# Attention over two K/V caches: the second cache's output weights in 128 partitions by heads, two more K tiles in halves, and the end of the last V reordered

## The chip, the cores and the metric

One core of one Trainium2 chip. The time is device microseconds (us) of a run. The kernel before takes 2613.69 us (median of 4 runs, 2612.04 to 2615.51). Each run lists its granted clock, and all profiles used here were taken in the fast state. In the profile, PE is the matmul engine, PEld its weight loads, DVE is VectorE, ACT is ScalarE, and SPq is the queue from which all large transfers are issued.

## The reference, cut to what matters

Two independent decode steps, A and B, with one query token and caches of their own. Each does:

```python
B, Sq, D = 8, 1, 1024;  H, Sk, Dh = 32, 4096, 128
q = (x @ wq).reshape(B, Sq, H, Dh).transpose(0, 2, 1, 3)
scores = einsum("bhqd,bhkd->bhqk", q, k_cache) * Dh ** -0.5
p = softmax(scores)
o = einsum("bhqk,bhkd->bhqd", p, v_cache)
out = o.transpose(0, 2, 1, 3).reshape(B, Sq, H * Dh) @ wo      # wo: 4096 x 1024
# result: concatenate([A's out, B's out], axis=-1)
```

Every byte of K and V is read once: 1074 MB, plus 34 MB of weights. All inputs are bfloat16.

Of the kernel before, what the change touches and what calls it, by code (L numbers as in the profile page):

```python
# [5 lines left out]
ALU = mybir.AluOpType  # L6
AX = mybir.AxisListType
BF16 = mybir.dt.bfloat16
FP32 = mybir.dt.float32
# [80 lines left out]
def _build_kernel(nc, caches, out):  # L90
# [6 lines left out]
    HQ = 8  # L97
# [16 lines left out]
    with es:  # L114
# [19 lines left out]
        pe = sb("pe", [128, T], BF16)  # L134
        PM = sb("PM", [128, T, HQ], BF16)
        accS = sb("accS", [128, 512], BF16)
        rl = sb("rl", [128, B], FP32)
        rl8 = sb("rl8", [128, B * HQ], FP32)
        on_sb = sb("on_sb", [128, H, B], BF16)
        on8 = sb("on8", [128, HQ, B], BF16)  # L140
        orow = sb("orow", [128, DT], BF16)

        red_ps = [ps(f"red{i}") for i in range(4)]
# [41 lines left out]

        opT, opMul, opEacc, opRed, opRmax, opNgm, opExp = {}, {}, {}, {}, {}, {}, {}
        opPV, opAcc, opExt, opQb, opQbc, opQ, opQs, opLsum = {}, {}, {}, {}, {}, {}, {}, {}
        opNorm, opProj, opUse, opPM = {}, {}, {}, {}
        last = {"misc": None, "norm": None}
        outs = []  # L190

# [14 lines left out]
        put("k", 0)  # L206
        put("wq", 1, 2)
        for n in range(NQ - 1):
            if n + 2 < NQ:
                put("k", n + 1)  # L210
            else:
                put("k", n + 1, cuts=((0, NR // 2), (NR // 2, NR)))
            put("v", n, 2)

            for c in range(NC):
                if n == done_at(c, NC, HB, B) + 1:
                    put("wo", c)
                    late[n + 2] = c
        put("v", NQ - 1, cuts=((0, NR // 2),))
        put("wo8", 0, 2)  # L220
        plan.append(("v", NQ - 1, ((NR // 2, 3 * NR // 4), (3 * NR // 4, 7 * NR // 8), (7 * NR // 8, NR))))
        tenant = [None, None, ("x", 0)]
        before = []
        for kind, n, cuts in plan:
# [4 lines left out]

        def tile_of(kind, n):  # L230
            return ring[:, slot[(kind, n)], :]

        def wo_rows(c):
            return MB * (HB if c < NC - 1 else HB - 1)

        def load_tiles():
            while issued[0] < len(plan):
                kind, n, cuts = plan[issued[0]]
                prev = before[issued[0]]
                dep = None  # L240
                if prev not in (None, (kind, n)):
                    dep = opUse.get(prev)
                    if dep is None:
                        return
                to = tile_of(kind, n)
                key = ("t", slot[(kind, n)])
                if kind in ("k", "v"):
                    blk, b = divmod(n, B)
                    c, hb = divmod(blk, HB)
                    from_ = caches[c][1 if kind == "k" else 2][b, hb * HQ:(hb + 1) * HQ].rearrange("u (m t) d -> (u m) (t d)", m=MP)  # L250
                    for r0, r1 in cuts or ((0, NR),):
                        cols = slice(r0 * CT * Dh, r1 * CT * Dh)
                        op = dma(to[:, cols], from_[:, cols], (kind + "l", r0) if cuts else key, [dep])
                        for r in range(H):
                            opT[(kind, n, r)] = op
                elif kind == "wq":
                    opT[(kind, n)] = dma(to[:, 0:DC * H * Dh], caches[n][3].rearrange("(p k) n -> p (k n)", k=DC), key, [dep])
                elif kind == "wo":
                    rows = wo_rows(n)
                    opT[(kind, n)] = dma(to[0:rows, 0:H * D], caches[n][4][0:rows * H, :].rearrange("(p r) n -> p (r n)", r=H),  # L260
                                         key, [dep])
                else:
                    opT[(kind, n)] = dma(to[:, 0:HQ * D].rearrange("p (j n) -> p j n", j=HQ),
                                         caches[-1][4][(H - HQ) * Dh:, :].rearrange("(j p) n -> p j n", p=128), key, [dep])
                issued[0] += 1


# [104 lines left out]
        def make_acc(n):  # L372
            opAcc[n] = add("act", lambda e: e.activation(accS[:], pv_ps[:], ACTF.Copy), [opPV[n], _at(opExt, n - 1)])  # L373

        def last_block(n):
            return n // B == NB - 1

        def make_ext(n):
            blk, b = divmod(n, B)
            hb = blk % HB  # L380
# [9 lines left out]

            def emit_last(e):
                for i in range(4):
                    x = e.matmul(o_ps[:, HQ * b:HQ * (b + 1)], accS[:, i * 128:(i + 1) * 128],  # L393
                                 E[:, i, PH - 1:].rearrange("p (j u) -> p j u", u=PH)[:, :, 0], start=(i == 0), stop=(i == 3))
                return x
            opExt[n] = add("pe", emit_last if last_block(n) else emit,
                           [opAcc[n], c_E, opLsum.get("rl"), last["norm"]] + (list(opQs.values()) if n == 0 else []))

        def make_lsum(blk):
            hb = blk % HB  # L400

            def emit(e):
                return e.matmul(o_ps[MB * hb:MB * (hb + 1), H * B:H * B + B], own_m[:].rearrange("p j u -> p (j u)"),
                                rsum[:, blk % 2, :], start=True, stop=True, tile_position=(0, MB * hb))

            def emit_last(e):
                for j in range(HQ):
                    x = e.matmul(o_ps[:, 64 + B * j:64 + B * (j + 1)], own_m[:, j, 0:1].to_broadcast([128, 128]),
                                 rsum[:, blk % 2, :], start=True, stop=True)
                return x  # L410
            n = blk * B + B - 1
            opLsum[blk] = add("pe", emit_last if blk == NB - 1 else emit, [opExp[n], c_own, last["norm"]])
            if blk == NB - 1:
                opLsum["rl"] = add("dve", lambda e: e.reciprocal(rl8[:], o_ps[:, 64:64 + B * HQ]), [opLsum[blk]])

        def make_norm(c):
            rows = slice(0, wo_rows(c))
            rec = add("dve", lambda e: e.reciprocal(rl[rows, :], o_ps[rows, H * B:H * B + B]),
                      [opExt[done_at(c, NC, HB, B)]] + [opLsum[blk] for blk in range(c * HB, c * HB + wo_rows(c) // MB)])
            opNorm[c] = last["norm"] = add("dve", lambda e: e.tensor_tensor(  # L420
                on_sb[rows, :, :].rearrange("p r b -> p b r"), o_ps[rows, 0:H * B].rearrange("p (b r) -> p b r", b=B),
                rl[rows, :].unsqueeze(2).to_broadcast([rows.stop, B, H]), ALU.mult), [rec, opProj.get(c - 1)])

        def make_proj(c):
            w = tile_of("wo", c)
            rows = slice(0, wo_rows(c))

            def emit(e):
                for r in range(H):
                    for q in range(NT):  # L430
                        x = e.matmul(proj[32 * q:32 * q + B, 0:DT], on_sb[rows, r, :], w[rows, r * D + q * DT:r * D + (q + 1) * DT],  # L431
                                     start=(r == 0), stop=(c < NC - 1 and r == H - 1), tile_position=(0, 32 * q))
                return x
            opProj[c] = opUse[("wo", c)] = add("pe", emit, [opNorm[c], opT[("wo", c)], c_proj] + outs)
            if c < NC - 1:
                make_out(c, opProj[c])

        def make_proj_last(norm):
            w = tile_of("wo8", 0)
            alone = ("wo", NC - 1) not in slot  # L440

            def emit(e):
                for j in range(HQ):
                    for q in range(NT):
                        x = e.matmul(proj[32 * q:32 * q + B, 0:DT], on8[:, j, :], w[:, j * D + q * DT:j * D + (q + 1) * DT],
                                     start=(alone and j == 0), stop=(j == HQ - 1), tile_position=(0, 32 * q))
                return x
            make_out(NC - 1, add("pe", emit, [norm, opT[("wo8", 0)], c_proj] + outs))

        def make_out(c, dep):  # L450
            ev = add("dve", lambda e: e.tensor_copy(orow[0:96 + B, :], proj[0:96 + B, 0:DT]), [dep] + outs[1:])
# [27 lines left out]
        for s in range(NS + LAG):  # L479
# [10 lines left out]
            if r == LAG - 1 and n >= 1:  # L490
                make_pm(n - 1)
            if r == 0 and n in late:
                make_proj(late[n])
            for k in range(4):
                v = pv_at.get(divmod(s - k, NR))
                if v is None:
# [5 lines left out]
                if k == 2:  # L502
                    make_ext(v)
                if k == 3:
                    for c in range(NC):
                        if v == done_at(c, NC, HB, B):
                            make_norm(c)
            if r == 2 and n % B == 0 and n >= 1:
                make_lsum(n // B - 1)

# [12 lines left out]
        make_pm(n)  # L523
        make_lsum(NB - 1)
        for g0, g1 in ((0, 8), (8, 12), (12, 14), (14, 16)):
            make_pv(n, g0 * RG // 16, g1 * RG // 16)
        make_acc(n)
        make_ext(n)
        norm = add("dve", lambda e: e.tensor_tensor(  # L529
            on8[:].rearrange("p j b -> p b j"), o_ps[:, 0:64].rearrange("p (b j) -> p b j", b=B),  # L530
            rl8[:].rearrange("p (j b) -> p b j", b=B), ALU.mult), [opLsum["rl"], opExt[n]])
        make_proj_last(norm)
        assert issued[0] == len(plan)

        counts = P.tokens()
# [58 lines left out]
```

## The kernel before: what the change and the argument touch

The caches are cut into 64 tiles of 8 MB (n = 0 to 63; 32 for A, 32 for B): one batch and 8 heads, in 128 partitions of 64 KB each. VectorE multiplies K tile n with the query and folds it in 8 chunks; PE sums further. The softmax of tile n and PV, the product of the probabilities with V tile n, are done while tile n + 1 is worked on. There are three slots of 64 KB per partition: two for K, in turn, and one for V. A load is issued only when the slot's last tenant is used up. The plan says in what order:

```python
        for n in range(NQ - 1):                      # NQ = 64, NR = 8 chunks
            if n + 2 < NQ:
                put("k", n + 1)
            else:
                put("k", n + 1, cuts=((0, NR // 2), (NR // 2, NR)))
            put("v", n, 2)
            for c in range(NC):
                if n == done_at(c, NC, HB, B) + 1:   # n = 32 for A, 56 for B
                    put("wo", c)                     # takes a K slot
                    late[n + 2] = c
        put("v", NQ - 1, cuts=((0, NR // 2),))
        put("wo8", 0, 2)                             # takes the V slot
        plan.append(("v", NQ - 1, ((NR // 2, 3 * NR // 4), (3 * NR // 4, 7 * NR // 8), (7 * NR // 8, NR))))
```

The weights wo of B are loaded in two parts, because its last 8 heads are finished only at the very end. The first part holds 24 heads in only 96 partitions of 64 KB; A's wo holds 32 heads in 128. In `load_tiles`:

```python
                if kind in ("k", "v"):
                    # ... (from_ is the tile in HBM)
                    for r0, r1 in cuts or ((0, NR),):
                        cols = slice(r0 * CT * Dh, r1 * CT * Dh)
                        op = dma(to[:, cols], from_[:, cols], (kind + "l", r0) if cuts else key, [dep])
                        for r in range(H):                     # every chunk, whatever the piece
                            opT[(kind, n, r)] = op
                # ... (wq)
                elif kind == "wo":
                    rows = wo_rows(n)                          # 128 for A, 96 for B
                    opT[(kind, n)] = dma(to[0:rows, 0:H * D],
                        caches[n][4][0:rows * H, :].rearrange("(p r) n -> p (r n)", r=H), key, [dep])
                else:                                          # wo8: the last 8 heads, rows of 2 KB
                    opT[(kind, n)] = dma(to[:, 0:HQ * D].rearrange("p (j n) -> p j n", j=HQ),
                        caches[-1][4][(H - HQ) * Dh:, :].rearrange("(j p) n -> p j n", p=128), key, [dep])
```

The main loop puts PV of tile n beside chunk 5 of K tile n + 1 (`pv_at = {(n + 1, 5): n ...}`). The end:

```python
        n = NQ - 1
        make_pm(n)
        make_lsum(NB - 1)
        for g0, g1 in ((0, 8), (8, 12), (12, 14), (14, 16)):
            make_pv(n, g0 * RG // 16, g1 * RG // 16)   # RG = 16; waits for opT of its last chunk
        make_acc(n)
        make_ext(n)
        # ... norm, product with wo8, output
```

## Time and profile before

| what | before |
|---|---|
| median time | 2613.69 us |
| span of the profiled execution | 2611.2 us |
| read from HBM | 1107.33 MB |
| VectorE busy | 85% |
| PE busy | 47% |

First, two lines of the page of the kernel before: what the transfers moved in 40 equal slices of 65 us, and the chain of waits that ended last, by engine.

```profile
GB/s 418 434 434 434 433 433 433 432 432 433 433 432 431 433 432 433 429 428 433 432 403 435 434 434 435 431 432 432 432 433 433 432 432 432 432 304 432 426 430 292
...
DMA 52%; DVE 44%; PE 2%; issue 1%; another core or an unknown queue 0%; SPq 0%; ACT 0%; DVEq 0%
```

Nearly every slice moves about 433 GB/s. Four stand out: the first, slice 20 (403; slices are counted from 0), slice 35 (304) and the last. The table of windows of the kernel before looks into the last three. Its columns are the stretch, its length, the busy time of each engine (PE, PEld, DVE, ACT and POOL, each with its count of instructions), the granted PE clock, the busy share of the DMA engines, and GB/s. It counts a descriptor where it starts, so a short stretch can show a little more or less than was moved in it.

```profile
1360.00:1368.00 8.00, 4.11 (x65) 2.13 (x66) 3.32 (x3) 0.00 (x0) 0.00 (x0) 0.80 0.57 213
2294.00:2336.00 42.00, 14.95 (x100) 4.59 (x100) 23.61 (x19) 0.88 (x2) 0.00 (x0) 0.58 1.00 225
2370.00:2490.00 120.00, 57.77 (x336) 16.66 (x336) 107.05 (x87) 4.61 (x13) 0.00 (x0) 0.59 1.00 431
2574.00:2584.00 10.00, 7.53 (x79) 2.58 (x77) 10.00 (x9) 0.60 (x1) 0.00 (x0) 0.84 0.40 126
2584.00:2590.00 6.00, 2.75 (x8) 1.30 (x9) 3.85 (x7) 0.60 (x2) 0.00 (x0) 0.50 1.04 390
```

The second line is wo of B: the DMA engines are fully busy (1.00) and yet move 225 GB/s, half of what the third line shows for ordinary tiles. The first and fourth lines are different in kind: there the engines are idle about half of the time (0.57 and 0.40), so the queue has run dry. The last line is mostly the 2 MB part of wo in rows of 2 KB, at 390 GB/s.

The timeline of the kernel before shows who waits. Columns: start, duration, engine, line, operation, out<-in, how many; in brackets the idle time ahead of it and what ended that.

```profile
1364.45 0.33 SPq L160 DMA_DIRECT2D ring<-in_B_k_cache_dram  x1
...
2278.68 0.33 SPq L160 DMA_DIRECT2D ring<-in_B_wo_dram  x1
2281.54 2.29 DVE L311 TENSOR_TENSOR ring<-ring,qbc 128x4096 bf16<-128x4096 bf16 x1 [3.99 <-DMA ring<-in_B_k_cache_dram]
...
2319.59 0.33 SPq L160 DMA_DIRECT2D ring<-in_B_k_cache_dram  x1
...
2355.63 2.29 DVE L311 TENSOR_TENSOR ring<-ring,qbc 128x4096 bf16<-128x4096 bf16 x1 [38.02 <-DMA ring<-in_B_k_cache_dram]
...
2580.45 0.38 SPq L160 DMA_DIRECT2D ring<-in_B_wo_dram  x1
...
2600.73 5.17 PE L365 MATMUL pv<-ring,PM 128*32 128x512 bf16 x64 [8.01 <-DMA ring<-in_B_v_cache_dram]
2605.94 0.60 ACT L373 ACTIVATE accS<-pv 128x512 bf16<-128x512 f32 x1 [16.86 <-PE pv L365]
...
2607.46 1.05 PE L445 MATMUL proj<-ring,on 128*8 128x256 bf16 x32 [0.60 <-DVE on L529]
```

VectorE waits about 4 us for each K tile (here K57, at 2281.54), and 38.02 us for K58, which was queued behind wo. At the end, all 64 matmuls of PV of the last V run after its last piece has landed.

### The profile page before, as it was taken

Reading aid. Unit: us, or ns where it says so; the run is one execution under the profiler, and the core shown is the slowest. Engines: PE = TensorE matmul, PEld = TensorE weight load, DVE = VectorE, ACT = ScalarE, POOL = GpSimd, SP = SyncE. Lnnn points to the kernel's source line nnn. Section 1 sums busy time; section 2 is a strip of 40 time slices with the busy share of each in tenths; the row PEclk is TensorE's granted clock in tenths of the full one; section 3 lists DMA queues with packets and bytes.
Section 4 is the critical chain, followed back from the end, with each engine's and each line's share of the span. In section 5 each row is a group of like instructions: output and inputs, shape, how many; then the busy total and the mean of one; then the engine's idle time right before and its main releaser. Section 6 shows DMA issues by size and latency. Waiting matters only on the chain.

```text
span 2611.2 us, 18455 instructions
## 1 busy us (share of the span) xinstructions
PE 1221.1 (47%) x8046; PEld 371.0 (14%) x8046; DVE 2221.5 (85%) x1805; ACT 105.2 (4%) x273; POOL 5.7 (0%) x23
## 2 busy tenths in 40 slices
PE   2454554454454444455453544544544544533454
PEld 0111111111111111111111111111111111111111
DVE  3898889889889889889886998898898898848896
ACT  1100000000000000000000000000000000000000
POOL 0000000000000000000000000000000000000000
PEclk7665665665665665665565656656656656655666
DMA  9999999999999999999999999999999999999997
GB/s 418 434 434 434 433 433 433 432 432 433 433 432 431 433 432 433 429 428 433 432 403 435 434 434 435 431 432 432 432 433 433 432 432 432 432 304 432 426 430 292
DMA packets 20833, 1108.55 MB, mean 425 GB/s; under 512 B 2272, under 2 KB 2336, under 8 KB 3376
## 3 DMA queue, kind: packets, MB, share of 16 engines
q1 hardware_dynamic: 20656, 1107.32, 99.1%
q8 instruction: 63, 1.03, 0.2%
q14 instruction: 18, 0.15, 0.0%
q10 hardware_dynamic: 96, 0.05, 0.0%
HBM read 1107.33 MB, written 0.03 MB: 424 GB/s over the span
## 4 chain that ended last, share of the span: by engine, by line
DMA 52%; DVE 44%; PE 2%; issue 1%; another core or an unknown queue 0%; SPq 0%; ACT 0%; DVEq 0%
DMA ring<-in_B_k_cache_dram 26%; DMA ring<-in_A_k_cache_dram 25%; DVE ring L311 23%; DVE ring L316 12%; DVE s_sb L333 6%; DVE PM L353 3%; PE red L325 2%; DMA ring<-in_B_v_cache_dram 1%; DVE rmax L339 1%; PE pv L365 0%; DVE rtmp L341 0%; DVE ngm L344 0%; SPq L160 0%; DVE on_sb L420 0%
## 5 line engine op out<-in xcount | busy, mean ns | idle before, releaser
L311 DVE TENSOR_TENSOR ring<-ring,qbc 128x4096 bf16<-128x4096 bf16 x512 | 1169.3, 2284 | 351.8 <-DMA ring<-in_B_k_cache_dram 187.2
L325 PE MATMUL red<-ring,ident 128*128 128x512 bf16 x2048 | 834.4, 553 | 1334.7 <-DVE ring L316 1334.0
L316 DVE TENSOR_TENSOR ring<-ring 128x2048 bf16<-128x2048 bf16 x512 | 618.4, 1208 | 0.1
L325 PEld LDWEIGHTS red<-ring,ident 128*128 128x128 bf16 x2048 | 202.5, 120 | 1871.0 <-DVE ring L316 1606.0
L333 DVE TENSOR_REDUCE s_sb<-red 128x32 f32<-128x512 f32 x512 | 348.6, 681 | 1.4 <-PE red L325 1.4
L365 PE MATMUL pv<-ring,PM 128*32 128x512 bf16 x4096 | 320.7, 469 | 8.0 <-DMA ring<-in_B_v_cache_dram 8.0
L353 DVE TENSOR_TENSOR PM<-pe,own_h 128x2048 bf16<-128x2048 bf16 x64 | 146.2, 2284 | 0.7 <-ACT pe L347 0.7
L365 PEld LDWEIGHTS pv<-ring,PM 128*32 128x32 bf16 x4096 | 113.5, 114 | 223.2 <-issue 174.4
L347 ACT ACTIVATE pe<-s_sb,ngm 128x256 bf16<-128x256 f32 x64 | 32.5, 509 | 1032.7 <-DVE ngm L344 1032.7
L373 ACT ACTIVATE accS<-pv 128x512 bf16<-128x512 f32 x64 | 38.2, 597 | 851.5 <-PE pv L365 851.5
L301 ACT ACTIVATE qbc<-misc 128x128 bf16<-128x128 f32 x64 | 17.8, 278 | 580.5 <-PE misc L296 580.5
L386 PE MATMUL o<-accS,E 128*32 128x32 bf16 x896 | 31.7, 177 | 0.0
L386 PEld LDWEIGHTS o<-accS,E 128*32 128x32 bf16 x896 | 25.9, 94 | 23.7 <-ACT accS L373 13.1
L339 DVE TENSOR_REDUCE rmax<-s_sb 128x1 f32<-128x256 f32 x64 | 26.9, 420 | 2.2
L296 PE MATMUL misc<-q_sb,selb 8*32 8x128 bf16 x512 | 26.1, 294 | 1.2 <-ACT q_sb L284 1.2
L431 PE MATMUL proj<-ring,on_sb 128*8 128x256 bf16 (+1 forms) x256 | 12.5, 384 | 18.1 <-DMA ring<-in_B_wo_dram 16.7
L341 DVE TENSOR_SCALAR rtmp<-half,rmax 128x32 f32<-128x32 f32 x64 | 15.4, 241 | 2.3
L296 PEld LDWEIGHTS misc<-q_sb,selb 8*32 8x32 bf16 x512 | 9.3, 103 | 54.4 <-issue 54.4
L344 DVE TRANSPOSE_TENSOR_REDUCE ngm<-rtmp 128x1 f32<-128x32 f32 x64 | 13.5, 211 | 2.2
L275 PE MATMUL o<-ring,xT 128*8 128x512 bf16 x64 | 7.2, 627 | 11.0 <-DMA ring<-in_A_wq_dram 11.0
L529 DVE TENSOR_TENSOR on<-o,rl 128x64 bf16<-128x64 f32 x1 | 0.4, 436 | 13.7 <-PE o L393 13.7
L347 ACT ACTIVATION_READ_ACCUMULATOR pe<-s_sb,ngm 128x1 f32 x64 | 11.9, 187 | 0.0
(38 smaller groups left out, 56.5 us busy)
## 6 DMA issues: line engine op xcount, KB each, us to landing
ring<-in_B_k_cache_dram SPq DMA_DIRECT2D x2, 4096.0 KB, 36.7
ring<-in_B_v_cache_dram SPq DMA_DIRECT2D x1, 4096.0 KB, 32.1
ring<-in_B_wo_dram SPq DMA_DIRECT2D x1, 2048.0 KB, 10.4
ring<-in_B_v_cache_dram SPq DMA_DIRECT2D x1, 2048.0 KB, 14.8
ring<-in_B_v_cache_dram SPq DMA_DIRECT2D x2, 1024.0 KB, 17.6
ring<-in_A_k_cache_dram SPq DMA_DIRECT2D x32, 41.6
ring<-in_A_v_cache_dram SPq DMA_DIRECT2D x32, 27.4
ring<-in_B_k_cache_dram SPq DMA_DIRECT2D x31, 41.3
```

What stands on the lines that cost most here:

```text
L296: x = e.matmul(misc[32 * g:32 * (g + 1), 0:Dh], selb[rows, b, i, :], q_sb[rows, c, j * Dh:(j + 1) * Dh], start=(i == 0), stop=(i == 1), ti ...
L301: "act", lambda e: e.activation(qbc[:, n % 2, :], misc[:, 0:Dh], ACTF.Copy),
L311: opMul[s] = add("dve", lambda e: e.tensor_tensor(v, v, qbc[:, n % 2, :].unsqueeze(1).to_broadcast([128, CT, Dh]), ALU.mult), [opT[("k", n ...
L316: return add("dve", lambda e: e.tensor_tensor(v[:, :, 0:64], v[:, :, 0:64], v[:, :, 64:128], ALU.add), [opMul[s]])
L325: i = e.matmul(dst, ident[:], v[:, :, j, :], start=(j == 0), stop=(j == 3))
L333: opRed[s] = add("dve", lambda e: e.tensor_reduce(s_sb[:, n % 2, r * CT:(r + 1) * CT], red_ps[s % 4][:, :].rearrange("p (t w) -> p t w", w ...
L339: opRmax[n] = add("dve", lambda e: e.tensor_reduce(rmax[:], s_sb[:, n % 2, :], AX.X, ALU.max), [opRed[NR * n + NR - 1]])
L347: opExp[n] = add("act", lambda e: e.activation(pe[:], s_sb[:, n % 2, :], ACTF.Exp, bias=ngm[:, n % 2:n % 2 + 1], scale=scale, accum_out=rs ...
L353: opPM[n] = add("dve", lambda e: e.tensor_tensor(PM[:], pe[:].unsqueeze(2).to_broadcast([128, T, HQ]), own_h[:].unsqueeze(1).to_broadcast( ...
L365: i = e.matmul(pv_ps[32 * q:32 * (q + 1), :], PM[:, t:t + 4, :].rearrange("p t j -> p (t j)"), v[:, t * Dh:(t + 4) * Dh], start=(g == 0), ...
L373: opAcc[n] = add("act", lambda e: e.activation(accS[:], pv_ps[:], ACTF.Copy), [opPV[n], _at(opExt, n - 1)])
L386: x = e.matmul(o_ps[MB * hb:MB * (hb + 1), H * b:H * (b + 1)], E[:, i, PH - 1 - u:PH - 1 - u + MB], accS[:, i * 128 + H * u:i * 128 + H * ...
```

## The change

The intent: let B's first 24 heads of wo reach all 128 partitions (one row of 2 KB per head and partition); have the K tile beside each wo (K33, K57) begun on its first half, so that its slot is free sooner; put three quarters of the last V, not half, ahead of the last wo; and really wait for pieces singly. The core of the diff, with cuts:

```diff
-            if n + 2 < NQ:
-                put("k", n + 1)
-            else:
-                put("k", n + 1, cuts=((0, NR // 2), (NR // 2, NR)))
+            early = n == NQ - 2 or n + 1 in [done_at(c, NC, HB, B) + 2 for c in range(NC)]
+            put("k", n + 1, cuts=((0, NR // 2), (NR // 2, NR)) if early else None)
...
-        put("v", NQ - 1, cuts=((0, NR // 2),))
-        put("wo8", 0, 2)
-        plan.append(("v", NQ - 1, ((NR // 2, 3 * NR // 4), (3 * NR // 4, 7 * NR // 8), (7 * NR // 8, NR))))
+        put("v", NQ - 1, cuts=((0, NR // 2), (NR // 2, 3 * NR // 4)))
+        put("wo_last", 0, 2)
+        plan.append(("v", NQ - 1, ((3 * NR // 4, 7 * NR // 8), (7 * NR // 8, NR))))
...
-                        for r in range(H):
+                        for r in range(r0, r1):
                             opT[(kind, n, r)] = op
...
+                    heads = slice(0, H - HQ) if kind == "wo" else slice(H - HQ, H)
+                    cols = (heads.stop - heads.start) * D
+                    opT[(kind, n)] = dma(to[:, 0:cols].rearrange("p (h n) -> p h n", n=D),
+                                         caches[-1][4][heads.start * Dh:heads.stop * Dh, :].rearrange("(h p) n -> p h n", p=128), key, [dep])
...
-            make_pv(n, g0 * RG // 16, g1 * RG // 16)
+            make_pv(n, g0, g1)
```

RG is 16, so the last pair of lines changes nothing: PV was cut in the same four pieces before. What makes them wait singly is `range(r0, r1)`; before, each later piece overwrote the landing of all chunks. The rest of the diff follows from the new layout: all four head blocks of B now use the form of unpacking, sum and normalization that only the last block had.

More of the change, by code (lines that the diff above doesn't have):

```diff
@@ L136, in _build_kernel @@
         accS = sb("accS", [128, 512], BF16)
-        rl = sb("rl", [128, B], FP32)
-        rl8 = sb("rl8", [128, B * HQ], FP32)
+        rl = sb("rl", [128, B * HQ], FP32)
         on_sb = sb("on_sb", [128, H, B], BF16)
-        on8 = sb("on8", [128, HQ, B], BF16)
         orow = sb("orow", [128, DT], BF16)
@@ L187, in _build_kernel @@
         opPV, opAcc, opExt, opQb, opQbc, opQ, opQs, opLsum = {}, {}, {}, {}, {}, {}, {}, {}
-        opNorm, opProj, opUse, opPM = {}, {}, {}, {}
+        opNorm, opProj, opUse, opPM, opRl = {}, {}, {}, {}, {}
         last = {"misc": None, "norm": None}
@@ L231, in tile_of @@
             return ring[:, slot[(kind, n)], :]
-        def wo_rows(c):
-            return MB * (HB if c < NC - 1 else HB - 1)
         def load_tiles():
@@ L257, in load_tiles @@
                     opT[(kind, n)] = dma(to[:, 0:DC * H * Dh], caches[n][3].rearrange("(p k) n -> p (k n)", k=DC), key, [dep])
-                elif kind == "wo":
-                    rows = wo_rows(n)
-                    opT[(kind, n)] = dma(to[0:rows, 0:H * D], caches[n][4][0:rows * H, :].rearrange("(p r) n -> p (r n)", r=H),
-                                         key, [dep])
-                else:
-                    opT[(kind, n)] = dma(to[:, 0:HQ * D].rearrange("p (j n) -> p j n", j=HQ),
-                                         caches[-1][4][(H - HQ) * Dh:, :].rearrange("(j p) n -> p j n", p=128), key, [dep])
+                elif kind == "wo" and n < NC - 1:
+                    opT[(kind, n)] = dma(to[:, 0:H * D], caches[n][4].rearrange("(p r) n -> p (r n)", r=H), key, [dep])
+                else:
+                    heads = slice(0, H - HQ) if kind == "wo" else slice(H - HQ, H)
+                    cols = (heads.stop - heads.start) * D
+                    opT[(kind, n)] = dma(to[:, 0:cols].rearrange("p (h n) -> p h n", n=D),
+                                         caches[-1][4][heads.start * Dh:heads.stop * Dh, :].rearrange("(h p) n -> p h n", p=128), key, [dep])
                 issued[0] += 1
@@ L373, in make_acc @@
             opAcc[n] = add("act", lambda e: e.activation(accS[:], pv_ps[:], ACTF.Copy), [opPV[n], _at(opExt, n - 1)])
-        def last_block(n):
-            return n // B == NB - 1
         def make_ext(n):
@@ L392, in emit_last @@
                 for i in range(4):
-                    x = e.matmul(o_ps[:, HQ * b:HQ * (b + 1)], accS[:, i * 128:(i + 1) * 128],
+                    x = e.matmul(o_ps[:, HQ * (hb * B + b):HQ * (hb * B + b + 1)], accS[:, i * 128:(i + 1) * 128],
                                  E[:, i, PH - 1:].rearrange("p (j u) -> p j u", u=PH)[:, :, 0], start=(i == 0), stop=(i == 3))
                 return x
-            opExt[n] = add("pe", emit_last if last_block(n) else emit,
-                           [opAcc[n], c_E, opLsum.get("rl"), last["norm"]] + (list(opQs.values()) if n == 0 else []))
+            opExt[n] = add("pe", emit_last if blk // HB == NC - 1 else emit,
+                           [opAcc[n], c_E, opRl.get(blk), last["norm"]] + (list(opQs.values()) if n == 0 else []))
         def make_lsum(blk):
@@ L407, in emit_last @@
                 for j in range(HQ):
-                    x = e.matmul(o_ps[:, 64 + B * j:64 + B * (j + 1)], own_m[:, j, 0:1].to_broadcast([128, 128]),
+                    x = e.matmul(o_ps[:, HQ * B * HB + B * (HQ * hb + j):HQ * B * HB + B * (HQ * hb + j + 1)], own_m[:, j, 0:1].to_broadcast([128, 128]),
                                  rsum[:, blk % 2, :], start=True, stop=True)
@@ L411, in make_lsum @@
             n = blk * B + B - 1
-            opLsum[blk] = add("pe", emit_last if blk == NB - 1 else emit, [opExp[n], c_own, last["norm"]])
-            if blk == NB - 1:
-                opLsum["rl"] = add("dve", lambda e: e.reciprocal(rl8[:], o_ps[:, 64:64 + B * HQ]), [opLsum[blk]])
-        def make_norm(c):
-            rows = slice(0, wo_rows(c))
-            rec = add("dve", lambda e: e.reciprocal(rl[rows, :], o_ps[rows, H * B:H * B + B]),
-                      [opExt[done_at(c, NC, HB, B)]] + [opLsum[blk] for blk in range(c * HB, c * HB + wo_rows(c) // MB)])
-            opNorm[c] = last["norm"] = add("dve", lambda e: e.tensor_tensor(
-                on_sb[rows, :, :].rearrange("p r b -> p b r"), o_ps[rows, 0:H * B].rearrange("p (b r) -> p b r", b=B),
-                rl[rows, :].unsqueeze(2).to_broadcast([rows.stop, B, H]), ALU.mult), [rec, opProj.get(c - 1)])
@@ L424, in make_proj, with make_norm @@
-        def make_proj(c):
-            w = tile_of("wo", c)
-            rows = slice(0, wo_rows(c))
+            c = blk // HB
+            opLsum[blk] = add("pe", emit_last if c == NC - 1 else emit, [opExp[n], c_own, last["norm"]])
+            if c == NC - 1:
+                k = HQ * B
+                opRl[blk] = add("dve", lambda e: e.reciprocal(rl[:], o_ps[:, (HB + hb) * k:(HB + hb + 1) * k]), [opLsum[blk]])
+        def make_norm(c, n):
+            if c < NC - 1:
+                rec = add("dve", lambda e: e.reciprocal(rl[:, 0:B], o_ps[:, H * B:H * B + B]),
+                          [opExt[n]] + [opLsum[blk] for blk in range(c * HB, (c + 1) * HB)])
+                opNorm[c] = last["norm"] = add("dve", lambda e: e.tensor_tensor(
+                    on_sb[:].rearrange("p r b -> p b r"), o_ps[:, 0:H * B].rearrange("p (b r) -> p b r", b=B),
+                    rl[:, 0:B].unsqueeze(2).to_broadcast([128, B, H]), ALU.mult), [rec, opProj.get(c - 1)])
+                return
+            hb = n // B % HB
+            k = HQ * B
+            opNorm[(c, hb)] = last["norm"] = add("dve", lambda e: e.tensor_tensor(
+                on_sb[:, HQ * hb:HQ * (hb + 1), :].rearrange("p j b -> p b j"),
+                o_ps[:, hb * k:(hb + 1) * k].rearrange("p (b j) -> p b j", b=B),
+                rl[:].rearrange("p (j b) -> p b j", b=B), ALU.mult), [opRl[n // B], opExt[n], opProj.get(c - 1)])
@@ new lines, in make_proj @@
+        def make_proj(c, heads=None):
+            if c < NC - 1:
+                w, key, norm, steps, end, first = tile_of("wo", c), ("wo", c), opNorm[c], range(H), True, True
+            else:
+                kind = "wo" if heads.start == 0 else "wo_last"
+                norm = opNorm[(c, heads.stop // HQ - 1)]
+                key = (kind, c if kind == "wo" else 0)
+                w, steps, end = tile_of(*key), heads, heads.stop == H
+                first = heads.start == 0 or HB == 1
@@ L428, in emit @@
             def emit(e):
-                for r in range(H):
+                for r in steps:
                     for q in range(NT):
-                        x = e.matmul(proj[32 * q:32 * q + B, 0:DT], on_sb[rows, r, :], w[rows, r * D + q * DT:r * D + (q + 1) * DT],
-                                     start=(r == 0), stop=(c < NC - 1 and r == H - 1), tile_position=(0, 32 * q))
-                return x
-            opProj[c] = opUse[("wo", c)] = add("pe", emit, [opNorm[c], opT[("wo", c)], c_proj] + outs)
@@ L435, in make_proj @@
-            if c < NC - 1:
+                        col = (r - steps.start) * D + q * DT
+                        x = e.matmul(proj[32 * q:32 * q + B, 0:DT], on_sb[:, r, :], w[:, col:col + DT],
+                                     start=(first and r == steps.start), stop=(end and r == H - 1), tile_position=(0, 32 * q))
+                return x
+            opProj[c] = opUse[key] = add("pe", emit, [norm, opT[key], c_proj] + outs)
+            if end:
                 make_out(c, opProj[c])
-        def make_proj_last(norm):
-            w = tile_of("wo8", 0)
-            alone = ("wo", NC - 1) not in slot
-            def emit(e):
-                for j in range(HQ):
-                    for q in range(NT):
-                        x = e.matmul(proj[32 * q:32 * q + B, 0:DT], on8[:, j, :], w[:, j * D + q * DT:j * D + (q + 1) * DT],
-                                     start=(alone and j == 0), stop=(j == HQ - 1), tile_position=(0, 32 * q))
-                return x
-            make_out(NC - 1, add("pe", emit, [norm, opT[("wo8", 0)], c_proj] + outs))
@@ L492, in _build_kernel @@
             if r == 0 and n in late:
-                make_proj(late[n])
+                make_proj(late[n], range(0, H - HQ))
             for k in range(4):
@@ L504, in _build_kernel @@
                 if k == 3:
-                    for c in range(NC):
-                        if v == done_at(c, NC, HB, B):
-                            make_norm(c)
+                    c = v // B // HB
+                    if v == done_at(c, NC, HB, B) or (c == NC - 1 and v % B == B - 1):
+                        make_norm(c, v)
             if r == 2 and n % B == 0 and n >= 1:
@@ L525, in _build_kernel @@
         for g0, g1 in ((0, 8), (8, 12), (12, 14), (14, 16)):
-            make_pv(n, g0 * RG // 16, g1 * RG // 16)
+            make_pv(n, g0, g1)
         make_acc(n)
         make_ext(n)
-        norm = add("dve", lambda e: e.tensor_tensor(
-            on8[:].rearrange("p j b -> p b j"), o_ps[:, 0:64].rearrange("p (b j) -> p b j", b=B),
-            rl8[:].rearrange("p (j b) -> p b j", b=B), ALU.mult), [opLsum["rl"], opExt[n]])
-        make_proj_last(norm)
+        make_norm(NC - 1, n)
+        make_proj(NC - 1, range(H - HQ, H))
         assert issued[0] == len(plan)
```

## The prediction

> **What bounds the kernel now.** Transfers. The page's slices show about 433 GB/s almost everywhere; VectorE idles about 4 us per K tile (4.0 us before the tile that lands at 2281.5, released by its DMA). Time is saved only where transfers run below 433 GB/s. The table of windows shows three such places besides the start:
>
> 1. 2294–2336 us: 225 GB/s. This is wo of the second cache, 96 partitions of 64 KB: (433-225)x42/433 = 20 us lost. VectorE idles from 2317.6 to 2355.6, until the next K tile lands. The Trainium skill ("SBUF — State Buffer", "Door 1: The DMA port swizzle") says that DMA bandwidth depends on how many of 16 ports the partitions reach, and that 0..63 reach only the 8 even ones. The trace agrees in kind: half rate here, full rate for the first cache's wo in 128 partitions.
> 2. 1360–1368 us: 213 GB/s, 4 us lost. The first cache's wo takes a K slot and the next K is issued late (1364.45): the queue has run dry.
> 3. 2574–2584 us: 126 GB/s, 7 us lost. The last 2 MB of wo wait for the slot of the next to last V, free at 2580.45, while the queue holds only half of the last V before it.
>
> After the last V piece lands (2600.6) comes a bare tail of 10.5 us, of which PV of the whole last V is 5.2: each piece's landing overwrites that of all chunks, so K halves and V pieces aren't waited for singly.
>
> **What the change does.**
> - wo of 24 heads goes into 128 partitions, in rows of 2 KB. The old 2 MB block has such rows already: 390 GB/s in 2584–2590. I estimate 6.3 MB in 15.5–16.5 us in place of about 35. K58's issue then waits for K57's use; with K57 in halves VectorE starts it 4 us sooner and frees it at about 2315, as wo ends. Gain 18.5 us.
> - K33 in halves: VectorE starts up to 5 us sooner, the next K is issued at about 1360. Gain 3 us.
> - K63 in halves, three quarters of the last V before the last wo: the slot is free at 2576, the queue holds work until 2584, the hole vanishes. Gain 6.5 us.
> - PV by pieces: after the last piece 8 of 64 matmuls are left, 0.7 of 5.2 us. Gain 4.5 us.
> - Added: per block 16 small sum matmuls (3.6 us of PE), a reciprocal (0.56) and a multiply (0.44), three times more; hidden in the slack.
>
> Sum 32.5 us, all on the critical path: what follows each place is bound by transfers and only shifts.
>
> **Predicted: 2581 us**, 8 in 10 between 2575 and 2589. Faster by over 2%: 0.02; within 2%: 0.97; slower: 0.01.
>
> **What would show it.** Windows: wo of the second cache at about 400 GB/s and 16 us long; VectorE's wait for the next K about 20 us in place of 38; Timeline at the end: the wo piece issued about 26 us after the last K lands, no hole in the transfers, PV of the last V in four stretches, last landing to end about 6 us.
>
> **What would make it wrong.** 2 KB rows slower over 3072 descriptors than over 1024 (234 GB/s, the old block's mean from first to last row, would cost 10 us); VectorE freeing K57 later than wo's end; PV of the last V pushed behind the sums on PE.

## The result, and the profile after

The changed kernel takes 2583.27 us (median of 4 runs, 2582.40 to 2583.98): 30.4 us less. The ratio to before is 0.9883, 95% interval 0.9866 to 0.99. A ratio is the mean time of one kernel's fast runs over that of the other's of the same rounds, so not quite the ratio of the medians quoted. The gain is clear of noise, and 2583 lies within the predicted 2575 to 2589.

The same two lines of the page, of the changed kernel:

```profile
GB/s 422 437 426 435 435 431 431 436 429 435 433 430 435 434 430 426 435 435 433 428 430 427 435 430 434 436 426 435 434 430 428 432 436 428 429 411 434 427 429 369
...
DMA 51%; DVE 46%; PE 2%; issue 1%; SPq 0%; ACT 0%; DVEq 0%
```

Slice 20 now has 430, slice 35 has 411. The windows of the changed kernel, at the same places (the end has moved forward):

```profile
1360.00:1368.00 8.00, 2.34 (x48) 1.48 (x52) 0.00 (x0) 0.00 (x0) 0.00 (x0) 0.50 1.01 401
2294.00:2310.00 16.00, 10.21 (x88) 3.35 (x84) 16.00 (x14) 0.88 (x2) 0.00 (x0) 0.73 0.98 364
2310.00:2316.00 6.00, 1.50 (x16) 0.62 (x20) 1.50 (x2) 0.00 (x0) 0.00 (x0) 0.75 0.89 331
2547.00:2557.00 10.00, 7.93 (x75) 2.72 (x76) 10.00 (x9) 0.60 (x1) 0.00 (x0) 0.75 0.96 413
2562.00:2568.00 6.00, 3.61 (x17) 3.41 (x16) 3.86 (x5) 0.60 (x2) 0.00 (x0) 0.50 1.04 394
```

The dry stretch at the first wo is gone but for a rest (401), B's wo takes each DMA engine about 17 us (192 rows of 88 ns in the trace) in place of 30 (6 runs of 5.0 us), and a small hole follows it (331, DMA engines 0.89 busy). There is no hole before the last wo (413). The timeline of the changed kernel:

```profile
1359.88 0.33 SPq L158 DMA_DIRECT2D ring<-in_B_k_cache_dram  x1
...
2278.58 0.38 SPq L158 DMA_DIRECT2D ring<-in_B_wo_dram  x1
...
2312.62 0.34 SPq L158 DMA_DIRECT2D ring<-in_B_k_cache_dram  x1
...
2335.74 2.29 DVE L305 TENSOR_TENSOR ring<-ring,qbc 128x4096 bf16<-128x4096 bf16 x1 [24.25 <-DMA ring<-in_B_k_cache_dram]
...
2555.86 0.38 SPq L158 DMA_DIRECT2D ring<-in_B_wo_dram  x1
...
2568.10 5.31 PE L359 MATMUL pv<-ring,PM 128*32 128x512 bf16 x56
...
2574.70 0.61 PE L359 MATMUL pv<-ring,PM 128*32 128x512 bf16 x8 [1.29 <-DMA ring<-in_B_v_cache_dram]
2575.37 0.60 ACT L367 ACTIVATE accS<-pv 128x512 bf16<-128x512 f32 x1 [10.83 <-PE pv L359]
...
2576.88 1.05 PE L439 MATMUL proj<-ring,on_sb 128*8 128x256 bf16 x32 [0.60 <-DVE on_sb L420]
```

VectorE's wait for K58 is 24.25 us, not 38.02. Only 8 matmuls of PV are left after the last landing, 0.61 us of them.

The trace also records each of the 16 completion increments of a transfer. A tile may be used when the last one is in, so the sum of the gain is best taken over these last increments. All numbers are us; "rerun" is the changed kernel once more, run x9 below:

| event | before | changed | rerun | gained up to here (changed / rerun) |
|---|---|---|---|---|
| K34, behind A's wo | 1387.5 | 1385.0 | 1385.0 | 2.5 / 2.5 |
| K56, 22 tiles later | 2242.8 | 2241.5 | 2241.5 | 1.3 / 1.3 |
| K58, behind B's wo | 2355.6 | 2335.7 | 2336.8 | 19.9 / 18.8 |
| K63, last half | 2550.1 | 2530.4 | 2530.5 | 19.7 / 19.6 |
| last piece of V63 | 2600.6 | 2574.7 | 2574.8 | 25.9 / 25.8 |
| end of the span | 2611.2 | 2580.7 | 2581.7 | 30.5 / 29.5 |

So B's wo brought 18.6 us in the one profile and 17.5 in the other (at K63 the two agree again: 18.4 and 18.3), the transfers at the end 6.2, and PV by pieces 4.6 (3.7 in the rerun). A's wo brought 2.5 at once, of which 1.3 was left at K56. The 0.9 us by which the two tails differ (6.0 and 6.9 us after the last landing) is mostly the granted PE clock: the last product's 32 matmuls took 1.05 us at 1.00 in the one profile and 1.88 us at 0.54 to 0.50 in the rerun. The Trainium skill, "TensorE: Matmul & The Clock Gate", "Part 1: The HAM clock gate", describes such a halving by how busy PE has been; the two profiles agree in the factor (1.00 against 0.54 to 0.50). What set it off in the rerun alone isn't shown.

### The profile page after: what moved, and what is told of

Its sections match the earlier page's. It is cut to its first block, busy times and chain, and to the rows that moved or that the text cites. A ratio compares the mean times of both kernels' runs of the same rounds, so it can differ in the third digit from the quotient of the medians.

```text
span 2580.7 us, 17905 instructions
## 1 busy us (share of the span) xinstructions
PE 1219.7 (47%) x7768; PEld 374.6 (15%) x7768; DVE 2221.8 (86%) x1809; ACT 105.2 (4%) x273; POOL 5.7 (0%) x23
## 4 chain that ended last, share of the span: by engine, by line
DMA 51%; DVE 46%; PE 2%; issue 1%; SPq 0%; ACT 0%; DVEq 0%
DMA ring<-in_A_k_cache_dram 26%; DMA ring<-in_B_k_cache_dram 24%; DVE ring L305 24%; DVE ring L310 12%; DVE s_sb L327 6%; DVE PM L347 3%; PE red L319 2%; DVE rmax L333 1%; DMA ring<-in_B_v_cache_dram 1%; DVE rtmp L335 0%; DVE ngm L338 0%; PE pv L359 0%; SPq L158 0%; DVE rl L407 0%; DVE on_sb L414 0%
## 5 line engine op out<-in xcount | busy, mean ns | idle before, releaser
L341 ACT ACTIVATE pe<-s_sb,ngm 128x256 bf16<-128x256 f32 x64 | 32.5, 508 | 1008.0 <-DVE ngm L338 1008.0
L377 PE MATMUL o<-accS,E 128*32 128x32 bf16 x512 | 18.1, 177 | 0.0
L290 PEld LDWEIGHTS misc<-q_sb,selb 8*32 8x32 bf16 x512 | 9.2, 103 | 54.7 <-issue 54.7
L377 PEld LDWEIGHTS o<-accS,E 128*32 128x32 bf16 x512 | 14.8, 94 | 13.6 <-ACT accS L367 8.1
L439 PE MATMUL proj<-ring,on_sb 128*8 128x256 bf16 x256 | 12.1, 372 | 9.4 <-DMA ring<-in_A_wo_dram 5.8
L399 PEld LDWEIGHTS o<-rsum,own_m 128*128 128x128 f32 x64 | 14.5, 333 | 4.4 <-ACT pe L341 3.3
L399 PE MATMUL o<-rsum,own_m 128*128 128x8 f32 x64 | 13.8, 355 | 2.4 <-ACT pe L341 2.4
```

The lines of the kernel that those rows point to most:

```text
L290: x = e.matmul(misc[32 * g:32 * (g + 1), 0:Dh], selb[rows, b, i, :], q_sb[rows, c, j * Dh:(j + 1) * Dh], start=(i == 0), stop=(i == 1), ti ...
L341: opExp[n] = add("act", lambda e: e.activation(pe[:], s_sb[:, n % 2, :], ACTF.Exp, bias=ngm[:, n % 2:n % 2 + 1], scale=scale, accum_out=rs ...
L377: x = e.matmul(o_ps[MB * hb:MB * (hb + 1), H * b:H * (b + 1)], E[:, i, PH - 1 - u:PH - 1 - u + MB], accS[:, i * 128 + H * u:i * 128 + H * ...
L399: x = e.matmul(o_ps[:, HQ * B * HB + B * (HQ * hb + j):HQ * B * HB + B * (HQ * hb + j + 1)], own_m[:, j, 0:1].to_broadcast([128, 128]), rs ...
```

## The experiments

All were run in 5 rounds and in three calls: x1 to x4 on one chip, then x5 to x8 and x9 to x12 on another. Times are medians. The kernel before took 2613.0 us; the changed kernel was run again (2583.66).

| run | time, us | ratio to before |
|---|---|---|
| changed kernel | 2583.27 | 0.9883 |
| x1 landing by pieces alone | 2604.44 | 0.9969 |
| x2 K33 and K57 whole | 2587.95 | 0.9905 |
| x3 old order of the last V | 2586.54 | 0.9899 |
| x4 PV of the last V in one | 2588.25 | 0.9906 |
| x5 wo in runs of 48 KB | 2582.15 | 0.9882 |
| x6 all K in halves | 2587.93 | 0.9903 |
| x7 all K in halves, 48 KB | 2586.69 | 0.9899 |
| x8 96 partitions, rows of 2 KB | 2602.18 | 0.9959 |
| x9 changed kernel again | 2583.66 | 0.9887 |
| x10 K released sooner | 2584.06 | 0.9888 |
| x11 x10 with runs of 48 KB | 2581.79 | 0.988 |
| x12 PV later alone | 2584.05 | 0.9889 |

The 95% intervals of the ratios are about 0.0015 to either side; the runs of one kernel agree within 3 us at most, in most kernels within about 1. Differences under 1 us are not read.

### What halved the rate of B's wo: 96 partitions, or runs of 64 KB (x8)

The changed kernel, with the same bytes in the same short rows, but into 96 partitions (wrong result):

```diff
+                    if kind == "wo":
+                        opT[(kind, n)] = dma(to[0:96, 0:H * D].rearrange("p (h n) -> p h n", n=D),
+                                             caches[-1][4][heads.start * Dh:heads.stop * Dh, :].rearrange("(h p) n -> p h n", p=96), key, [dep])
+                    else:
```

> The changed kernel with the same 6 MB of wo in rows of 2 KB, 32 to a partition, but into 96 partitions (wrong result on purpose). Theory (the number of partitions is what halved the rate, not the row length): wo at about 210 GB/s, the next K's landing 17 to 19 us later, time about 2601. Rival (64 KB runs were slow by their length or their place in memory): wo at about 380 GB/s, time about 2583.

Measured 2602.18 us, 18.9 over the changed kernel. The stretches of wo in the table of windows of x8:

```profile
2294.00:2310.00 16.00, 10.00 (x64) 2.87 (x68) 16.00 (x14) 0.14 (x1) 0.00 (x0) 0.53 1.00 205
2310.00:2316.00 6.00, 2.91 (x32) 1.05 (x24) 1.19 (x2) 0.60 (x1) 0.00 (x0) 0.98 1.07 213
```

205 GB/s against 364 in the changed kernel's same stretch, the engines fully busy in both. The rival falls: it is the 96 partitions that halve the rate, not the length of the runs. The Trainium skill, "SBUF — State Buffer", "Door 1: The DMA port swizzle (why `[64,N]` ≈ `[32,N]`)", puts partitions 0..63 on the 8 even ports of 16, at an asymptote of about 218 GB/s, and 64..127 on the odd ones. It has no row for 96; the runs put it at that same rate. The count of ports reached, on which the prediction leaned, does not explain this: by the page's map 64..95 already reach all eight odd ports. That 96 partitions halve the rate is shown; why they do stays open.

### Is the next K held by VectorE's use of the tile beside wo (x2, x5)

x2 takes the halves of K33 and K57 back, leaving those of K63:

```diff
-            early = n == NQ - 2 or n + 1 in [done_at(c, NC, HB, B) + 2 for c in range(NC)]
+            early = n == NQ - 2
```

> The changed kernel with the K tiles next to both wo blocks (33 and 57) whole again, the last K still in halves. Theory (VectorE's use of these tiles sets when the next K is issued): 2.9 us lost at the first wo and about 4 us at the second, about 2590, and the hole after the second wo grows by 4 us. Rival (behind the second wo the transfer itself is the limit): only 2.9 us lost, about 2586.

Measured 2587.95 us, 4.7 slower, between the two. In the trace, K34 lands 3.1 us later than in the changed kernel (1388.1), K56 1.5 us later, and K58 5.7 us later (2341.4). VectorE stands idle for 3.83 us ahead of K57, and not at all in the changed kernel. So K57's halves are worth 4.2 us (5.7 less 1.5; against the rerun below 3.1), about the 4 us of the theory, and it is K33's gain of 3 us that had halved by then.

x5 loads wo in one run of 48 KB per partition, same bytes, 128 partitions (wrong result):

```diff
+                    if kind == "wo":
+                        opT[(kind, n)] = dma(to[:, 0:cols], caches[-1][4][heads.start * Dh:heads.stop * Dh, :].rearrange("(p r) n -> p (r n)", p=128), key, [dep])
+                    else:
```

> The changed kernel with the 24 heads of wo loaded as one run of 48 KB per partition, still 128 partitions and the same bytes (wrong result on purpose). Theory (the next K is issued when VectorE has used up the K tile before it, at 2312.6, whatever wo does): wo at about 430 GB/s, drained 2 us sooner, but time within 1 us of the changed kernel and the hole that much longer. Rival (the missing 2 us are the cost of 3072 rows of 2 KB): 2 to 2.5 us faster, about 2581.

Measured 2582.15 us, 1.1 under the changed kernel and 1.5 under its rerun x9 on the same chip: outside the 1 us of the theory, and short of the rival's 2 to 2.5. By the time alone the two can't be told apart. The windows show wo at 416 GB/s in 2294–2310 (changed: 364) and then 183 in 2310–2316 (changed: 331): what the faster load gained, the hole behind it took:

```profile
2294.00:2310.00 16.00, 10.87 (x84) 3.57 (x84) 16.00 (x13) 0.79 (x2) 0.00 (x0) 0.69 0.97 416
2310.00:2316.00 6.00, 4.02 (x48) 1.83 (x52) 1.25 (x2) 0.00 (x0) 0.00 (x0) 0.57 0.54 183
```

K58 lands at 2336.3, no sooner than in the changed kernel's two profiles (2335.7 and 2336.8), and the last piece of V63 only 0.4 to 0.5 us sooner (2574.3). So for the K behind wo the load's rate didn't count; K57's use did. The rest of the 1.1 to 1.5 us isn't traced.

### The end: order, halves or pieces (x1, x3, x4)

x1 is the kernel before with one line changed:

```diff
-                        for r in range(H):
+                        for r in range(r0, r1):
```

> The kernel before, with only this changed: each piece's landing is recorded for its own chunks, so the halves of the last K and the pieces of the last V are really waited for singly; wo, plan and order as before. Theory (tail gain is PV by pieces, 4.7 us, plus a last K begun 4 us sooner, which frees the slot for the last wo 4 us sooner and so takes 3.5 to 4 us of the hole): 8.5 us under before, about 2605. Rival (the hole closes only by the new order of V pieces): 4.7 us, about 2609.

x3 is the changed kernel with the old order of the last V:

```diff
-        put("v", NQ - 1, cuts=((0, NR // 2), (NR // 2, 3 * NR // 4)))
+        put("v", NQ - 1, cuts=((0, NR // 2),))
...
-        plan.append(("v", NQ - 1, ((3 * NR // 4, 7 * NR // 8), (7 * NR // 8, NR))))
+        plan.append(("v", NQ - 1, ((NR // 2, 3 * NR // 4), (3 * NR // 4, 7 * NR // 8), (7 * NR // 8, NR))))
```

> The changed kernel with the last wo again after the first half of the last V, not after three quarters. Theory (the halves of the last K close most of the hole, the order only the rest): 2 to 3 us slower than the changed kernel, about 2585.5. Rival (the order closes it all): 6.5 us slower, about 2590.

x4 is the changed kernel with PV of the last V in one:

```diff
-        for g0, g1 in ((0, 8), (8, 12), (12, 14), (14, 16)):
-            make_pv(n, g0, g1)
+        make_pv(n, 0, RG)
```

> The changed kernel with PV of the last V in one piece after its last landing. Theory: 64 matmuls of 81 ns after the landing in place of 8, 4.6 us slower, about 2588. Rival (PV by pieces overlaps nothing, since the sums' matmuls and the last product come late): under 2 us slower.

x1 measured 2604.44 us, 8.6 under before: one line brings 28% of the whole gain (8.6 of 30.4). Its last wo is issued at 2575.65, not 2580.45. The total is that of the theory, 8.5; in the profile, 5.2 of it lies in the landing of the last piece of V63 (2595.4) and 3.3 in the tail behind it. x3 measured 2586.54, 3.3 slower than the changed kernel, a little over the expected 2 to 3: from K63's last increment to V63's it takes 47.2 us (2530.6 to 2577.8), against 44.3 in the changed kernel and 50.5 before. So by x3 the halves of K63 bring 3.3 of the 6.2 us here and the order 2.9. In x1, which has the halves with the old order, the same stretch takes 45.8 us (2549.6 to 2595.4): by x1 the halves bring 4.7 and the order 1.5. The split is known only within that range; neither rival holds in either. x4 measured 2588.25, 5.0 slower, as expected: its 64 matmuls take 5.88 us after the last landing.

### Can more be had: VectorE further ahead (x6, x7)

x6 puts every K tile in halves:

```diff
-            early = n == NQ - 2 or n + 1 in [done_at(c, NC, HB, B) + 2 for c in range(NC)]
+            early = True
...
-                        op = dma(to[:, cols], from_[:, cols], (kind + "l", r0) if cuts else key, [dep])
+                        op = dma(to[:, cols], from_[:, cols], (kind + "l", r0 + (slot[(kind, n)] if kind == "k" else 0)) if cuts else key, [dep])
```

> The changed kernel with every K tile after the first in halves, with landing counters of their own by slot. Theory (VectorE may run further ahead, so the tile next to each wo is used up some 5 us sooner and no hole is left after either wo): 2 to 3 us faster, about 2580.5. Rival (VectorE is not what holds the next K): same within 1 us.

x7 is x6 with wo as in x5:

> All K in halves and wo in runs of 48 KB (wrong result on purpose). Theory (with VectorE out of the way the transfer is the limit, and 2 KB rows at 370 GB/s against 433 cost 2.5 us): 2 to 2.5 us under all K in halves with short rows. Rival (row length costs nothing): same as that within 1 us.

x6 missed: 2587.93 us, 4.7 slower, where 2 to 3 faster was expected. A line of the waits of x6 (200 to 1200 us of the span), and its timeline at B's wo, show why:

```profile
PE pv L359 <- DMA ring<-in_A_v_cache_dram: 113.0, 26, 5.3
```

```profile
2303.51 3.61 PE L359 MATMUL pv<-ring,PM 128*32 128x512 bf16 x32 [4.11 <-DMA ring<-in_B_v_cache_dram]
2307.05 1.69 PE L319 MATMUL red<-ring,ident 128*128 128x512 bf16 x4
```

PV of tile n stands in PE's order before the K sums of the later chunks of tile n + 1 (its first half before those of chunk 4). VectorE was further ahead, but V lands no sooner; so PE stood waiting for V in every tile (26 times, 113.0 us), with the K sums, and so the K slot, behind it. K58 was issued at 2312.54, no sooner than in the changed kernel. This tells why nothing was gained. Most of the loss came before: at K56 x6 is 3.7 us behind the changed kernel (2245.2 against 2241.5). The 16 completion increments of K56 lie 10.2 us apart there, against 5.8, and their mean is only 1.9 us behind. Why they lie further apart with every K in halves isn't shown. x7 (2586.69, 1.2 under x6) is inconclusive for the same reason: what it was to take out of the way was still there.

### K57 really released sooner (x9 to x12)

x10 puts only three K tiles up to each wo in halves, and PV one chunk later in the last two:

```diff
-            early = n == NQ - 2 or n + 1 in [done_at(c, NC, HB, B) + 2 for c in range(NC)]
+            early = n == NQ - 2 or n + 1 in [done_at(c, NC, HB, B) + 2 - i for c in range(NC) for i in range(3)]
...
-        pv_at = {(n + 1, 5): n for n in range(NQ - 1)}
+        pv_at = {(n + 1, 6 if n + 1 in [done_at(c, NC, HB, B) + 2 - i for c in range(NC) for i in range(2)] else 5): n for n in range(NQ - 1)}
```

with the landing counters of x6. x11 adds the long runs of x5 (wrong result), x12 has only the change of `pv_at`, and x9 is the changed kernel once more.

> The changed kernel itself, unaltered, as the control of this call: about 2583.3 us, with 4.5 to 5.4 us lost against full rate from 2270 to 2345 us and about 1 us from 1330 to 1400 us.

> The changed kernel with the three K tiles up to each wo (31 to 33, 55 to 57) in halves and PV one chunk later in the last two of them, so that PE doesn't stand waiting for V ahead of the K sums as it did with every K in halves. Theory (the moment at which tile 57, and 33, is used up sets the next K's issue): tile 57 used up at about 2308 in place of 2312.6 us, the hole after wo gone, 2 us gained there and 0.7 at the first wo, 2.5 to 3 us under the changed kernel. Rival (the loss there is all the cost of 2 KB rows): within 1 us of it.

> The kernel x10 with wo in runs of 48 KB (wrong result on purpose). Theory (once tile 57 is used up before wo is drained, the row length counts): 1 to 2.5 us under x10. Rival (row length never counts here): within 0.7 us of x10.

> The changed kernel with only PV one chunk later in the two tiles up to each wo, a control for x10. Theory: tile 57 used up about 1 us later, so 0 to 1.5 us slower than the changed kernel. Rival (x10's gain, if any, comes from PV's place): as much faster as x10.

x10 did what was expected of it on the spot. K57 is used up and K58 issued at 2307.42, and the hole behind wo is gone, as the window over wo and what follows it shows, first of the rerun x9, then of x10:

```profile
2296.00:2330.00 34.00, 16.98 (x184) 6.85 (x182) 15.52 (x12) 0.60 (x1) 0.00 (x0) 0.65 1.00 392
```

```profile
2296.00:2330.00 34.00, 14.13 (x177) 6.04 (x176) 10.16 (x9) 0.60 (x1) 0.00 (x0) 0.65 1.05 420
```

28 GB/s more over 34 us is 2.2 us of transfer at 433 GB/s. Yet the time is 2584.06 us, not under the rerun's 2583.66. The theory that closing the hole gains its length failed. The completion increments show where it went. For each tile: when the last of 16 increments came, how long after the first, and the mean of the 16.

| tile | before | x9 (rerun) | x10 | x11 |
|---|---|---|---|---|
| K34, last | 1387.5 | 1385.0 | 1385.6 | 1384.9 |
| K34, last after first | 1.8 | 3.4 | 6.2 | 5.9 |
| K34, mean | 1386.1 | 1382.7 | 1382.4 | 1381.7 |
| K58, last | 2355.6 | 2336.8 | 2335.8 | 2333.2 |
| K58, last after first | 6.0 | 2.1 | 5.7 | 5.1 |
| K58, mean | 2352.5 | 2335.1 | 2332.5 | 2330.2 |
| K63 second half, last | 2550.1 | 2530.5 | 2531.3 | 2528.7 |
| K63 second half, last after first | 4.1 | 1.9 | 4.8 | 5.6 |

The 16 parts of a transfer drift apart while the stream runs: in each of these profiles the distance from first to last grows from under 2 us to 5.6 to 6.0 us in the first 1000 us (K25). Where the queue runs dry, the parts that are ahead wait and those behind catch up: in the kernel before it falls from 5.5 to 1.8 us across the hole at A's wo, in x9 from 6.0 to 3.4 across a smaller one, and in x10, without a hole, it stays at 6.2. In x10 the mean part of K58 came 2.6 us sooner than in x9, the last part only 1.0, and at K63 nothing was left (the last part 0.8 later; of the 2.6 us of the mean, 1.6 were left, 2527.7 against 2529.3, and why that shrank is open). VectorE starts on the last part. So part of the hole had cost nothing: the part of the transfer that was last hardly waited in it. x12 shows the same from the other side: its later PV puts off the issue of V32 from 1317.35 (x9) to 1323.03, and that of V56 from 2272.55 to 2276.60. In both the mean increment comes 2.0 us later and the last only 0.4, and the distance falls to 2.3 and 2.1 us (x9: 6.0 and 4.9). The Trainium skill, "DMA: Bandwidth & Descriptors", "Why a DMA increments its semaphore by 16 and not by 1", says that the engines of a transfer finish independently and that only the full 16 means that all has landed; the trace agrees, and adds that the distance builds up.

x11 is 2.3 us faster than x10: with K57 out of the way, the length of the rows counts, as expected. x12 measured 2584.05, 0.4 over the rerun, so PV's later place gains nothing by itself. No correct version beats the changed kernel.

## Why the prediction was right or wrong, point by point

- **Total: right.** 2581 predicted, 2583.27 measured; a gain of 32.5 predicted, 30.4 measured. Nearly all that is missing is A's wo.
- **Three places, and what kind each is: right.** 96 partitions halve the rate (x8); the two other places were a dry queue (DMA engines 0.57 and 0.40 busy). The count of ports, by which the prediction explained the first, isn't shown (see x8).
- **B's wo: right.** Gain 18.5 predicted, 18.6 and 17.5 in two profiles. From K57's last increment to wo's it took 54.7 us before and 35.2 after (rerun: 35.4), V56 included; from there to K58's it took 19.4 before and 20.2 after (rerun: 21.2). So wo brought some 19.4, and the hole behind it took back 0.8 to 1.8. Both costs that the prediction had named as risks were real but small: rows of 2 KB ran slower than estimated (17.0 us on each engine, not 15.5 to 16.5: 88 ns mean for a row, not the 81 to 84 of the old block's best), and K57 was used up at 2312.6, when 8 of wo's 16 increments were in. Without either, x11 lands K58 at 2333.2, 2.5 to 3.6 us sooner.
- **A's wo: mis-sized.** 3 us predicted; 2.5 at the next landing, 1.3 at K56. The step that failed is the prediction's "what follows each place is bound by transfers and only shifts". It took the lost mean rate for lost time. Measured by the last part, 0.6 of the 3.1 us mean gain at K34 (1386.1 to 1383.0) was lost at once, because the parts stayed further apart (3.1 against 1.8 us). A further 1.2 us went in the 22 tiles after; the mean gain shrank too (2240.0 to 2237.8, 2.2 at K56), and why is open. x1, which up to here is the kernel before, shows the same shrinking (2.6 us at K34, 1.4 at K56), and so does x2 from the other side (3.1 and 1.5).
- **The end: right.** Transfers 6.5 predicted, 6.2 measured, PV by pieces 4.5 predicted, 4.6 and 3.7 measured (x4: 5.0). The prediction gave the 6.5 to halves and order together; x3 splits it into 3.3 and 2.9, x1 into 4.7 and 1.5. PV ran in two stretches (56 and 8 matmuls), not four: the sums of the last block kept PE until 2568.1, and the third of the four pieces landed at 2572.2, just as PE came to it.
- **What was added: right.** The sums (16 per block, 3.58 us of PE) and the reciprocals show in no wait that matters.

## What to carry to other kernels

A transfer into 96 partitions can run at half the rate of one into 128, with the DMA engines fully busy all the while: look at GB/s, not at the busy share, and pay for a finer layout if that fills the partitions. When a load takes a slot out of a ring, ask when the tile that holds the other slot is used up, since that and not the load may issue the next one; and check what stands ahead of it in an engine's order before letting another engine run further ahead. A hole in the transfers can be worth less than its length, because the part of the stream that is behind catches up in it: count in last landings, not in mean rate.

## What the Trainium skill lacked or had wrong

- "SBUF — State Buffer", "Door 1: The DMA port swizzle": no row for 96 partitions, and the count of ports doesn't give their rate, since 0..95 reach all 16. Here 205 to 225 GB/s, the rate that the page gives for 64, against 416 to 433 for 128 partitions in long runs.
- "DMA: Bandwidth & Descriptors", "Specifications", gives 512 B and more as enough for line rate. Here rows of 2 KB into 128 partitions ran at 363 to 364 GB/s where runs of 48 KB ran at 416 to 426 (the stretch 2294–2310 of x10 and the changed kernel, and of x5 and x11), and cost 2.3 us in 6 MB once nothing else held the next load (x10 against x11).
- The same page says that a transfer's engines finish independently and that a bulk load runs at the pace of its slowest engine. It doesn't say that the parts of back-to-back transfers drift apart, here from under 2 us to 5.5 us, nor that they come together where the queue runs dry (5.5 to 1.8 us), so that a hole costs less than its length. What makes them drift stays open.
